# Pooled attention, then a gated two-layer net: late softmax sums of two heads in one matmul, and the engines' queues in another order

## The chip, the core and the metric

The kernel runs as one program on one core of a Trainium2 chip. Its engines are TensorE (PE, matmuls into PSUM), VectorE (DVE), ScalarE (ACT), GpSimd (POOL) and SyncE (SP, which issues the DMAs). They run side by side, each takes its own instructions in their order, and semaphores make one wait for another. The metric is the device time of a run in microseconds (us), as the median of several runs; lower is better. 0.3% of it is 2.6 us.

## What is computed

Four batches of eight heads of attention, 1152 keys, the queries averaged in pairs to 576; then every one of the 2304 rows of 512 numbers goes through a layer of 2048, a gate, and a layer back to 512. All is float32.

```
q_pool = q.reshape(B, H, S // 2, 2, D).mean(axis=3)         # B 4, H 8, S 1152, D 64
scores = (1 / sqrt(D)) * matmul(q_pool, k.transpose(0, 1, 3, 2))
attn = exp(scores - max(scores, axis=-1))
attn = attn / (sum(attn, axis=-1) + 1e-09)
x = matmul(attn, v)                                         # then rows of (B*S/2, H*D)
h = x @ w_in                                                # 512 -> 2048
out = (h * clip(h + 3.0, 0.0, 6.0) / 6.0) @ w_out           # 2048 -> 512
```

## The kernel before

**Groups and halves.** The attention is cut into 16 groups `g` (a batch and a pair of heads), and each group into two halves `h` of 288 queries. Within a half, `j` is the head of the pair. Scores stand with the keys on the 128 partitions, in nine blocks of 128 keys (`pqk`, L617, early groups `pv`, L613): a block is copied to SBUF by ACT, and DVE keeps the maximum over blocks (`m`). Groups 0 to 4 are "early" and use plain float32 scores; from group 5 on ("late") keys and queries are split in a high and a low part. The maximum over partitions goes through two small transposes on PE, `fold` and `spread` (L656 and L677 in the late form). Then DVE widens it (L649), subtracts it from the scores in three pieces a head (`s`, L688), ACT takes the exponential in place, POOL adds the nine blocks (`d`, L706), and PE multiplies with `v` (`pav`, L713, 36 matmul records a half).

**The late sums.** For each head, DVE's `turn_d` (L726) folds 288 sums of 128 partitions to 9 columns with 32 rows in each of four partition quarters. `sums` (L734) adds over the quarters with two matmuls into the same nine columns of PSUM: the matrix `same[:, 0]` puts head 0's total on partitions 0 to 63, `same[:, 1]` head 1's on 64 to 127. As float32 each is two records in the trace, four in all. Then, on DVE: `recip` (L762 adds 1e-9, L763 inverts), `widen_r` (L738), `divide` (L777). The tile `psr` that they work on takes the one PSUM buffer of tag `av` that the next half's `pav` needs.

**The net.** Its weights are split in two parts once, written to `w_d` in DRAM, and loaded again for each use (`w`, L375, half 0 for the first layer, half 1 for the second, three buffers each). x goes to DRAM as `xh_d` and `xl_d` (L791, "spill") and comes back by chunks of 256 rows (`mxmxh`, `mxmxl`, L382). A hidden step is 12 matmuls (`ph`, L392), then ACT, DVE (gate, L401), ACT and POOL; a projection step is 6 matmuls (`po`, L425). Six chunks of 16 steps run between the attention's matmuls; the last 768 rows run alone at the end: a chunk of 256 by `mxmxh` and `mxmxl`, and 512 rows in `last` (L907), for which the program's last part loads its weights by the same SP queue.

**The order.** Nothing is ordered by hand. `arrange` lists every step with a place in time, a cost on each engine that may run it, what it needs and which buffers it takes; `Order.run` walks through time and lets each free engine take the ready step with the least place. The constants at the top (`START`, `SLOPE`, `LAG`, `MLP`, `AT`, `ATL`, `PER`, `BIAS`, `CONV`, `CSTEP`, `STICK`) set the places; the costs stand in `arrange`. The resulting sequence is what the engines' queues hold: a queue waits at its next instruction, whatever stands behind it.

## Time and profile before

| | us |
| --- | --- |
| median of 3 runs | 880.97 |
| lowest and highest | 880.77, 883.16 |
| the profiled execution, its own time | 882.37 |
| span of its instructions | 880.6 |
| PE busy in the span | 841.0 |
| DVE, ACT, POOL busy | 671.9, 570.5, 496.5 |

The mean granted clock of PE is 0.99 of full speed. The profile shows the program in four parts: to about 175 us the early groups with the weights' conversion, then the late groups with six chunks of the net to about 707 us, then the end of the attention while the last chunk's x is under way, and from about 750 us the net alone.

### The profile page before, as it was taken

What the parts mean: (1) busy time and instruction counts of PE and PEld (TensorE: products, weight loads), DVE (VectorE), ACT (ScalarE), POOL (GpSimd) and SP (SyncE); (2) the same over time, 40 slices, a digit from 0 to 9 for tenths busy, and PEclk for the clock granted to TensorE, in tenths of its full rate; (3) what the DMA queues carried; (4) which work ended last, traced back from release to release, by engine and by line L of the source; (5) the groups of instructions that cost most, each with busy time, mean ns of one, the idle gap of its engine ahead of it and who ended that gap; (6) DMA issues with size and microseconds to landing.
All of it is one profiled execution on the core that took longest, in us unless ns stands there. A gap on an engine that the chain in (4) does not pass through costs nothing.

```text
span 880.6 us, 16285 instructions
## 1 busy us (share of the span) xinstructions
PE 841.0 (96%) x5712; PEld 653.7 (74%) x5712; DVE 671.9 (76%) x1313; ACT 570.5 (65%) x1203; POOL 496.5 (56%) x436
## 2 busy tenths in 40 slices
PE   4799999999999999999999999999999998999997
PEld 3445555577788887778888878888887876888886
DVE  4899999988988998888989887998888862222322
ACT  3779889886777786657767766776777652222222
POOL 2557775665768686828675767778676672000000
PEclk9899999999999999999999999999999999999999
DMA  9979596689787869969758778887767668533423
GB/s 244 318 215 284 176 287 219 226 276 322 273 258 253 252 242 282 299 206 311 242 188 259 243 239 273 288 239 258 243 240 250 216 211 265 186 120 120 144 96 96
DMA packets 114545, 206.06 MB, mean 234 GB/s; under 512 B 44576, under 2 KB 68128, under 8 KB 114464
## 3 DMA queue, kind: packets, MB, share of 16 engines
q1 hardware_dynamic: 113776, 203.65, 72.5%
q10 hardware_dynamic: 688, 1.38, 0.5%
q8 instruction: 45, 0.74, 0.3%
q14 instruction: 36, 0.29, 0.1%
HBM read 173.02 MB, written 31.98 MB: 233 GB/s over the span
## 4 chain that ended last, share of the span: by engine, by line
PE 71%; DVE 11%; DMA 7%; issue 5%; ACT 4%; POOL 1%; SPq 1%; DVEq 0%; POOLq 0%; ACTq 0%
PE ph L392 20%; PE po L425 15%; PE pav L713 12%; PE pqk L617 10%; PE pt L425 5%; DMA w<-w_d 4%; DVE m L635 4%; PE pv L613 3%; DVE s L688 2%; PE pt L591 1%; ACT s L522 1%; PE psr L744 1%; DVE kT L576 1%; DMA mxmxl<-xl_d 1%; DMA raw<-in_moe_w_in_dram 1%
## 5 line engine op out<-in xcount | busy, mean ns | idle before, releaser
L696 ACT ACTIVATE s<-s 128x864 f32<-128x864 f32 x192 | 177.5, 932 | 27.6 <-DVE s L688 25.9
L392 PE MATMUL ph<-mxmxh,w 128*128 128x256 f32 x896 | 182.4, 287 | 1.9 <-DVE r L401 1.0
L522 ACT COPY s<-pqk 128x288 f32<-128x288 f32 x396 | 145.4, 402 | 42.2 <-PE pqk L617 39.5
L688 DVE TENSOR_TENSOR s<-s,pst 128x864 f32<-128x864 f32 x167 | 172.0, 1042 | 0.5
L635 DVE TENSOR_TENSOR m<-pqk,m 128x288 f32<-128x288 f32 x308 | 137.3, 446 | 22.4 <-ACT s L522 14.8
L713 PE MATMUL pav<-s,vr 128*64 128x288 f32 x1152 | 153.4, 412 | 0.0
L392 PEld LDWEIGHTS ph<-mxmxh,w 128*128 128x128 f32 x896 | 147.4, 191 | 6.0 <-DVE r L401 2.5
L397 ACT ACTIVATE r<-ph,three 128x256 f32<-128x256 f32 (+1 forms) x128 | 64.0, 500 | 130.1 <-PE ph L392 124.0
L425 PE MATMUL po<-w,gh 128*128 128x512 f32 x448 | 140.3, 395 | 0.0
L401 DVE SCALAR_TENSOR_TENSOR r<-r,ph 128x256 f32<-128x256 f32 (+1 forms) x128 | 57.2, 447 | 97.6 <-ACT r L397 97.0
L392 PE MATMUL ph<-mxmxl,w 128*128 128x256 f32 x448 | 127.1, 284 | 1.0 <-DMA mxmxl<-xl_d 1.0
L410 POOL TENSOR_TENSOR gl<-r,gh 128x256 fp32r<-128x256 f32 x96 | 71.8, 748 | 92.2 <-ACT gh L405 88.0
L617 PE MATMUL pqk<-qh,kT 128*128 128x288 f32 x396 | 118.8, 315 | 2.1 <-ACT s L522 1.4
L713 PEld LDWEIGHTS pav<-s,vr 128*64 128x64 f32 x1152 | 77.3, 137 | 57.9 <-issue 10.7
L706 POOL TENSOR_TENSOR d<-s 128x864 f32<-128x864 f32 x44 | 90.3, 2053 | 51.5 <-ACT s L696 49.1
L617 PE MATMUL pqk<-ql,kT 128*128 128x288 f32 x396 | 111.6, 295 | 0.0
L425 PE MATMUL po<-w,gl 128*128 128x512 f32 x224 | 91.7, 409 | 6.8 <-DMA w<-w_d 4.7
L425 PEld LDWEIGHTS po<-w,gh 128*128 128x128 f32 x448 | 85.0, 190 | 14.6
L706 POOL TENSOR_TENSOR d<-d,s 128x864 f32<-128x864 f32 x44 | 90.3, 2053 | 1.7 <-ACT s L696 0.6
L392 PEld LDWEIGHTS ph<-mxmxl,w 128*128 128x128 f32 x448 | 85.7, 191 | 2.0 <-DMA mxmxl<-xl_d 1.2
L617 PEld LDWEIGHTS pqk<-qh,kT 128*128 128x128 f32 x396 | 75.1, 190 | 13.0 <-issue 3.1
L405 ACT CAST gh<-r 128x256 fp32r<-128x256 f32 (+1 forms) x128 | 55.8, 436 | 40.4 <-DVE r L401 37.4
(103 smaller groups left out, 1417.8 us busy)
## 6 DMA issues: line engine op xcount, KB each, us to landing
w<-w_d SPq DMA_DIRECT2D x224, 512.0 KB, 6.1
w_d<-scratch SPq DMA_DIRECT2D x32, 512.0 KB, 5.7
kr<-in_k_dram SPq DMA_DIRECT2D x32, 288.0 KB, 5.1
vr<-in_v_dram SPq DMA_DIRECT2D x16, 576.0 KB, 4.8
qr<-in_q_dram SPq DMA_DIRECT2D x15, 576.0 KB, 5.1
raw<-in_moe_w_in_dram SPq DMA_DIRECT2D x16, 512.0 KB, 4.9
raw<-in_moe_w_out_dram SPq DMA_DIRECT2D x16, 512.0 KB, 6.0
xh_d<-xh SPq DMA_DIRECT2D x32, 144.0 KB, 4.1
```

Source lines behind the costliest of these rows:

```text
L392: nc.tensor.matmul(ps, w[:, wi, cs], x[:, c, :], start=(m == 0), stop=(m == 3 * NCC - 1))
L397: nc.scalar.activation(out=r6, in_=ps, func=AF.Relu, bias=three)
L401: nc.vector.scalar_tensor_tensor(out=out, in0=r6, scalar=6.0, in1=ps, op0=ALU.min, op1=ALU.mult)
L410: on.tensor_tensor(out=gl, in0=r6, in1=gh.bitcast(F32), op=ALU.subtract)
L425: nc.tensor.matmul(o, g[:, ts], w[:, wi, :], start=(first and n == 0), stop=(last and n == 2))
L522: nc.scalar.copy(out=out, in_=in_)
L617: nc.tensor.matmul(ps[:, 0:HQ], kT[g][:, j, t, :], w[:, j, :], start=(m == 0), stop=(m == 1))
L635: nc.vector.tensor_tensor(out=m, in0=ps, in1=s0 if t == 1 else m, op=ALU.max)
L688: by[eng].tensor_tensor(out=s, in0=s, in1=m.unsqueeze(1).to_broadcast([P, KC, HQ]), op=ALU.subtract)
L696: nc.scalar.activation(out=s, in_=s, func=AF.Exp, scale=SCALE)
L706: by[eng].tensor_tensor(out=out, in0=x, in1=y, op=ALU.add)
L713: nc.tensor.matmul(av_t[g, h][j * D:(j + 1) * D, :], vr_t[g][:, j, t, :], s_t[g, h][:, j, t, :], start=(t == 0), stop=(t == KT - 1),)
```

## The change

Three things. `same` becomes one matrix of 128 by 128 that adds over the quarters for any column, and `sums` one matmul of 18 columns, nine of each head, so that every partition gets both heads' totals. `recip` adds 1e-9 to all 18 columns into a new tile, and inverts twice, on partitions 0 to 63 the nine columns of head 0, on 64 to 127 those of head 1. And all constants of the order are other numbers, with slightly other costs for some ten steps.

```diff
-        same = const.tile([P, 2, P], F32, name="same")
-        nc.vector.memset(same, 0.0)
-        for j in range(2):
-            nc.vector.tensor_reduce(
-                out=same[:, j, j * D:j * D + 32], in_=ident.rearrange("p (i k) -> p k i", k=32), axis=AX.X, op=ALU.add
-            )
-            nc.vector.tensor_copy(out=same[:, j, j * D + 32:j * D + 64], in_=same[:, j, j * D:j * D + 32])
+        same = const.tile([P, P], F32, name="same")
+        nc.vector.tensor_reduce(out=same[:, 0:32], in_=ident.rearrange("p (i k) -> p k i", k=32), axis=AX.X, op=ALU.add)
+        for i in range(1, 4):
+            nc.vector.tensor_copy(out=same[:, 32 * i:32 * (i + 1)], in_=same[:, 0:32])
...
-            for j in range(2):
-                nc.tensor.matmul(ps[:, HQ:HQ + NB], same[:, j], d[:, j], start=(j == 0), stop=(j == 1))
+            nc.tensor.matmul(ps[:, HQ:HQ + 2 * NB], same, d.rearrange("p j b -> p (j b)"), start=True, stop=True)
...
-            n, w = (P, NB) if g >= EARLY else (QP, 2 * TQ)
+            late = g >= EARLY
+            n, w = (P, NB) if late else (QP, 2 * TQ)
             den = d_t["r", g, h] = sm.tile([n, w], F32, tag=f"den{w}", name="den")
-            nc.vector.tensor_scalar(out=den, in0=d_t["p", g, h][:n, HQ:HQ + w], scalar1=EPS, scalar2=None, op0=ALU.add)
+            x = d_t["p", g, h][:n, HQ:HQ + 2 * w if late else HQ + w]
+            if late:
+                y = sm.tile([n, 2 * w], F32, tag="sum", name="sum")
+                nc.vector.tensor_scalar(out=y, in0=x, scalar1=EPS, scalar2=None, op0=ALU.add)
+                for j in range(2):
+                    nc.vector.reciprocal(out=den[j * D:(j + 1) * D], in_=y[j * D:(j + 1) * D, j * w:(j + 1) * w])
+                return
+            nc.vector.tensor_scalar(out=den, in0=x, scalar1=EPS, scalar2=None, op0=ALU.add)
             nc.vector.reciprocal(out=den, in_=den)
...
-ATL = (22.01, -2.54, -233.12, 551.12, 311.61, 236.17, 57.41, -176.29, 297.81, 167.8, 536.81, 237.72, 502.76, 92.46)
+ATL = (22.34, -3.63, -205.22, 577.83, 408.65, 315.01, 114.68, -312.66, 169.9, 228.56, 501.2, 268.78, 483.12, 159.04)
...
-                add(("rc", g, h), z, {"DVE": (345, 430)}, do("recip", g=g, h=h), [("de", g, h)])
+                add(("rc", g, h), z, {"DVE": (470, 560)}, do("recip", g=g, h=h), [("de", g, h)])
```

The new order shows at three places below. A row is an instruction, or some in a row, with its line (numbers differ by up to four in the new file), what it writes and reads, and the size of what it writes.

**SP's queue at the load of group 11's keys** (`kr`; `w` with a number are the net's weights, `xh_d` and `xl_d` the spill of a half). Before:

```order
L791 DMA xh_d<-xh 128x288
L791 DMA xl_d<-xl 128x288
L375 DMA w_5185<-w_d 128x1024
L506 DMA kr<-in_k_dram 128x9x64 x2
L375 DMA w_5218<-w_d 128x1024
L375 DMA w_5263<-w_d 128x1024
```

and now:

```order
L375 DMA w_5184<-w_d 128x1024
L375 DMA w_5214<-w_d 128x1024
L503 DMA kr<-in_k_dram 128x9x64 x2
L795 DMA xh_d<-xh 128x288
L795 DMA xl_d<-xl 128x288
L375 DMA w_5280<-w_d 128x1024
L375 DMA w_5301<-w_d 128x1024
```

The spill of a half stood two loads ahead of the keys and now stands right behind them, ahead of the weights. `w_5218` was for the second layer of the third chunk's step 9, `w_5280` is for that of step 8.

**DVE's queue at the last half of the attention**, from the widened maximum on (`pst<-pst`; `s` the three subtractions a head, `den`, `sum` and `psr<-den` the reciprocals of the half before, `x` its division, `r` a gate of the net). Before:

```order
L649 STREAM_TRANSPOSE pst<-pst 128x288
L688 TENSOR_TENSOR s<-s,pst 128x864 x3
L649 STREAM_TRANSPOSE pst<-pst 128x288
L688 TENSOR_TENSOR s<-s,pst 128x864 x2
L762 TENSOR_SCALAR den<-psr 128x9
L763 RECIPROCAL den<-den 128x9
L688 TENSOR_TENSOR s<-s,pst 128x864
L738 STREAM_TRANSPOSE psr<-den 128x288
L401 SCALAR_TENSOR_TENSOR r_9055<-r_9055,ph 128x256
L777 TENSOR_TENSOR x<-psr,x 128x288
```

and now:

```order
L646 STREAM_TRANSPOSE pst<-pst 128x288
L762 TENSOR_SCALAR sum<-psr 128x18
L764 RECIPROCAL den<-sum 64x9 x2
L401 SCALAR_TENSOR_TENSOR r_9045<-r_9045,ph 128x256
L734 STREAM_TRANSPOSE psr<-den 128x288
L685 TENSOR_TENSOR s<-s,pst 128x864
L781 TENSOR_TENSOR x<-psr,x 128x288
L685 TENSOR_TENSOR s<-s,pst 128x864 x2
L401 SCALAR_TENSOR_TENSOR r_9090<-r_9090,ph 128x256
L646 STREAM_TRANSPOSE pst<-pst 128x288
L685 TENSOR_TENSOR s<-s,pst 128x864 x3
```

The reciprocals of the half before, its division and a gate have moved from behind the subtractions to between the first of them.

**SP's queue at the end of the attention** (`last` the 512 rows, `out_dram` the sixth chunk's results; `w_9276` and `w_9278`, now `w_9297` and `w_9299`, are the net-alone part's weights for the first step's second layer and the second step's first layer). Before:

```order
L382 DMA mxmxl<-xl_d 128x4x256
L791 DMA xh_d<-xh 128x288
L791 DMA xl_d<-xl 128x288
L375 DMA w_9234<-w_d 128x1024
L907 DMA last<-xh_d 128x512
L907 DMA last<-xl_d 128x512
L375 DMA w_9276<-w_d 128x1024
L375 DMA w_9278<-w_d 128x1024
L439 DMA out_dram<-ob 64x512 x2
L439 DMA out_dram<-ob 32x512
L439 DMA out_dram<-ob 96x512
```

and now:

```order
L375 DMA w_9239<-w_d 128x1024
L795 DMA xh_d<-xh 128x288
L795 DMA xl_d<-xl 128x288
L375 DMA w_9297<-w_d 128x1024
L911 DMA last<-xh_d 128x512
L911 DMA last<-xl_d 128x512
L439 DMA out_dram<-ob 64x512 x2
L439 DMA out_dram<-ob 32x512
L439 DMA out_dram<-ob 96x512
L375 DMA w_9299<-w_d 128x1024
```

The weights of the first step's second layer have moved ahead of `last`, and those of the second step's first layer behind the four writes of results; the load of `mxmxl` stands some rows further ahead.

## Rows read from the trace of the kernel before

**Rows 1.** The page's part 1: each engine's busy time, share of the span, instructions.

```profile
PE 841.0 (96%) x5712; PEld 653.7 (74%) x5712; DVE 671.9 (76%) x1313; ACT 570.5 (65%) x1203; POOL 496.5 (56%) x436
```

**Rows 2.** Windows: stretch and length, busy time of each engine, clock, DMA.

```profile
175.00:200.00 25.00, 23.52 (x182) 18.07 (x183) 21.50 (x43) 19.48 (x43) 14.52 (x15) 0.93 0.85 278
200.00:700.00 500.00, 492.64 (x3419) 406.65 (x3419) 437.32 (x910) 356.15 (x826) 347.31 (x295) 1.00 0.80 257
700.00:760.00 60.00, 55.17 (x351) 44.14 (x347) 26.22 (x55) 23.17 (x46) 26.21 (x25) 1.00 0.68 220
...
380.00:400.00 20.00, 17.93 (x122) 14.55 (x121) 15.84 (x33) 12.75 (x28) 8.10 (x7) 0.91 0.83 252
```

**Rows 3.** Timeline of PE at 388: start, duration, instruction, [idle before <-releaser].

```profile
388.25 0.77 PE L425 MATMUL po<-w,gl 128*128 128x512 f32 x1 [2.08 <-POOL gl L410]
...
390.95 0.44 PE L617 MATMUL pqk<-qh,kT 128*128 128x288 f32 x1
```

**Rows 4.** Timeline of PE: the late sums of a half, and what follows.

```profile
717.52 0.51 PE L734 MATMUL psr<-dh,same 128*128 128x9 f32 x4
717.89 0.48 PE L425 MATMUL po<-w,gl 128*128 128x512 f32 x1
```

**Rows 5.** Groups by shape: line, instruction, count | busy us, mean ns | idle.

```profile
L734 PE MATMUL psr<-dh,same 128*128 128x9 f32 x88 | 11.2, 237 | 0.0
...
L677 PE MATMUL pst<-ident,mq 18*128 18x18 f32 x22 | 5.1, 233 | 0.0
...
L763 DVE RECIPROCAL den<-den 128x9 f32<-128x9 f32 x22 | 4.7, 216 | 0.8
```

**Rows 6.** Timeline of PE: last turns of group 10's keys, and a projection.

```profile
427.91 1.15 PE L557 MATMUL pt<-ident,kr 128*128 128x128 f32 x9
...
437.03 0.47 PE L425 MATMUL po<-w,gl 128*128 128x512 f32 x1 [0.32 <-DMA w<-w_d]
```

**Rows 7.** Timeline of SP's queue at the load of group 11's keys.

```profile
429.08 1.55 SPq L506 DMA_DIRECT2D kr<-in_k_dram  x2
430.68 6.11 SPq L375 DMA_DIRECT2D w<-w_d  x6
```

**Rows 8.** Chain that ended last: start, length, and whose work.

```profile
449.26 1.43 PE ph L392 x12
...
455.74 1.43 PE po L425 x6
458.31 4.52 PE pav L713 x36
```

**Rows 9.** Timeline of PE at the end of the attention.

```profile
706.76 0.30 PE L617 MATMUL pqk<-ql,kT 128*128 128x288 f32 x1
...
711.32 0.23 PE L677 MATMUL pst<-ident,mq 18*128 18x18 f32 x1
...
730.66 0.51 PE L734 MATMUL psr<-dh,same 128*128 128x9 f32 x4
...
748.77 0.28 PE L392 MATMUL ph<-mxmxh,w 128*128 128x256 f32 x1
```

**Rows 10.** Timeline of DVE in the last half of the attention.

```profile
712.12 2.98 DVE L688 TENSOR_TENSOR s<-s,pst 128x864 f32<-128x864 f32 x3
...
718.07 0.17 DVE L762 TENSOR_SCALAR den<-psr 128x9 f32<-128x9 f32 x1 [0.38 <-PE psr L734]
...
720.03 0.44 DVE L777 TENSOR_TENSOR x<-psr,x 128x288 f32<-128x288 f32 x1
...
728.95 0.47 DVE L726 TRANSPOSE_TENSOR_REDUCE dh<-d 128x9 f32<-128x288 f32 x1
```

**Rows 11.** Timeline of SP's queue at the end of the attention.

```profile
734.17 0.33 SPq L791 DMA_DIRECT2D xl_d<-xl  x1
...
739.57 0.32 SPq L907 DMA_DIRECT2D last<-xh_d  x1
...
743.24 2.26 SPq L439 DMA_DIRECT2D out_dram<-ob  x4
```

More of the change, by code (lines that the diff above doesn't have):

```diff
@@ L22 @@
 SWEEPS = ((0, 0, 8), (1, 0, 8), (0, 8, 16), (1, 8, 16), (2, 0, 16), (3, 0, 16), (4, 0, 16), (5, 0, 16))
-START = (297.45, 126.76, 394.29, 391.14, 380.14, 242.67, 333.14, 318.82)
-SLOPE = (-16.27, 2.59, -17.76, -9.21, 2.22, 26.51, 6.64, 17.68)
-LAG = 47.47
-MLP = (-344.5, 180.43, 24.29, -233.84)
-CONV = 259.96
-CSTEP = (428.74, 384.8)
+START = (246.01, 179.96, 358.36, 509.43, 415.86, 207.51, 251.46, 423.87)
+SLOPE = (-21.77, 9.37, -4.06, -18.53, 9.98, 26.0, 16.54, -0.66)
+LAG = 97.02
+MLP = (-392.54, 215.62, -17.55, -355.89)
+CONV = 309.52
+CSTEP = (368.54, 137.77)
 NEAR = 5
@@ L31 @@
 FCV = 12
-BIAS = (-117.79, -123.14, 79.41, -364.14, 39.25, 376.58)
+BIAS = (-634.41, -292.0, 59.75, -514.28, -65.55, 233.98)
 CUT = 8
-PER = (22.3, 20.22)
-AT = (216.76, -40.7, 3.26, 213.12, -263.52, 209.56, -146.85, 99.67, -205.13, 147.08, -190.26, -65.61, -218.54, 179.6)
-ATL = (22.01, -2.54, -233.12, 551.12, 311.61, 236.17, 57.41, -176.29, 297.81, 167.8, 536.81, 237.72, 502.76, 92.46)
+PER = (12.05, 21.32)
+AT = (287.65, -106.4, 1.62, 311.32, -328.57, 265.33, -319.67, 212.92, -55.41, 196.21, -167.72, -123.72, -327.69, 416.38)
+ATL = (22.34, -3.63, -205.22, 577.83, 408.65, 315.01, 114.68, -312.66, 169.9, 228.56, 501.2, 268.78, 483.12, 159.04)
 TAIL = 768
-STICK = 0.1993
+STICK = 0.2226
 CT = 256
@@ L179, in arrange @@
             if late:
-                add(("kl", g, c), z + 2 + c, {"DVE": (1130, 1130)}, do("keep_k", g=g, c=c), [("kh", g, c)], (), ("v" if g < NEAR else "s",))
+                add(("kl", g, c), z + 2 + c, {"DVE": (1178, 1160)}, do("keep_k", g=g, c=c), [("kh", g, c)], (), ("v" if g < NEAR else "s",))
         for h in range(NH if late else 1):
@@ L218, in arrange @@
                         p = (g, h)
-                        add(("tr", p), z + at[8], {"DVE": (665, 750)}, do("turn_m", u=p), [("mx", (g, h, n), KT - 1) for n in range(2)], (), ("m",))
+                        add(("tr", p), z + at[8], {"DVE": (700, 780)}, do("turn_m", u=p), [("mx", (g, h, n), KT - 1) for n in range(2)], (), ("m",))
                         add(("s1", p), z + at[2], {"PE": (110, 330, 0, "t")}, do("fold", u=p), [("tr", p)], ("st",))
-                        add(("s2", p), z + at[2], {"DVE": (430, 510)}, do("best", u=p), [("s1", p)])
-                        add(("s3", p), z + at[2], {"PE": (85, 300, 0, "t")}, do("spread", u=p), [("s2", p)])
+                        add(("s2", p), z + at[2], {"DVE": (485, 560)}, do("best", u=p), [("s1", p)])
+                        add(("s3", p), z + at[2], {"PE": (120, 320, 0, "t")}, do("spread", u=p), [("s2", p)])
                     if j:
                         for n in range(2):
-                            add(("tb", (g, h, n)), z + at[2] + n, {"DVE": (365, 450)}, do("widen_m", u=(g, h, n)),
+                            add(("tb", (g, h, n)), z + at[2] + n, {"DVE": (405, 498)}, do("widen_m", u=(g, h, n)),
                                 [("s3", p)] + [("su", (g, h, 0), c) for c in C3] * n)
@@ L242, in arrange @@
                 if late:
-                    add(("dt", u), z + at[7], {"DVE": (365, 450)}, do("turn_d", u=u), [("ad", u, 3)], () if j else ("dh",), ("d",))
+                    add(("dt", u), z + at[7], {"DVE": (392, 470)}, do("turn_d", u=u), [("ad", u, 3)], () if j else ("dh",), ("d",))
             y = z + at[5]
@@ L256, in arrange @@
             if late:
-                add(("de", g, h), z, {"PE": (200, 420, 0, "s")}, do("sums", g=g, h=h),
+                add(("de", g, h), z, {"PE": (190, 410, 0, "s")}, do("sums", g=g, h=h),
                     [("dt", (g, h, j)) for j in range(2)] + [("av", g, h, n)], ("av",), ("dh",))
-                add(("rc", g, h), z, {"DVE": (345, 430)}, do("recip", g=g, h=h), [("de", g, h)])
-                add(("rb", g, h), z, {"DVE": (365, 450)}, do("widen_r", g=g, h=h), [("rc", g, h)])
+                add(("rc", g, h), z, {"DVE": (470, 560)}, do("recip", g=g, h=h), [("de", g, h)])
+                add(("rb", g, h), z, {"DVE": (392, 482)}, do("widen_r", g=g, h=h), [("rc", g, h)])
             else:
```

## The prediction

> **What bounds the kernel now.** I read the page's busy times first: PE is busy for 841.0 of 880.6 us, the next engine, DVE, for 671.9 [rows 1]. So the time is PE's work and PE's waits, and the other engines count where PE waits for them. The windows say where it waits [rows 2]. From 200 to 700 us it is busy for 492.64 of 500, so 7.4 us are lost there; from 175 to 200, 1.5; from 700 to 760, 4.8. The worst of the middle is at 388 us, where PE stood for 2.08 us before a projection and then ran slow: the same score matmul that takes 0.30 takes 0.44 at 390.95 [rows 3], and the window from 380 to 400 has a granted clock of 0.91, near 1.8 us of 20 lost on top of the 2.07 of idleness [rows 2]. The early part, to 175 us, is no subject: all five queues hold the same rows in both kernels until the keys of group 5 are turned, but for the constants set up at the start, which lie under the first loads.
>
> All sums below are made on the profiled execution, span 880.6, own time 882.37. The median, 880.97, lies 0.4 above that span; I add the change of the span to the median.
>
> **The matmul.** Before, four records of the late sums take from 717.52 to 717.89, 0.37 us of PE's time [rows 4]; there are 22 halves (x88 records) [rows 5]. Now there are two records of 18 columns in place of four of 9. Do twice as many columns cost more? The trace has no such float32 product, but the nearest row, a small transpose of 18 columns, has a mean of 233 ns beside 237 for the 9 columns [rows 5], so the count of columns is not what costs here. I take half: 0.18 us each. The bounds are nothing saved, if 18 columns cost twice 9, and 0.2 each. Twenty of the 22 lie ahead of the last scores, where PE is the bound: 20 x 0.18 = **-3.6 us**. The last two stand in the end of the attention, where another chain decides (below): 0.
>
> The Trainium skill (TensorE: Matmul & The Clock Gate, Step-by-step: what each phase is for) says that streaming costs one cycle a column and that throughput is N cycles. By that rule alone one product of 18 columns would save nothing over two of 9, and the sum would be 3.6 us higher; the rows above, where 9 columns hold PE for about 90 ns a record, don't agree that columns are all.
>
> **The reciprocals.** DVE gets one more of 216 ns [rows 5] for each of 22 halves, on half the partitions each; bounds 0.1 and 0.22, so 2 to 5 us of DVE's time in all, I take 0.2 each. Behind it on DVE wait the widening, the division, and the maxima and subtractions of the next half; who waits in the end is the next `pav`, for the buffer that the division frees. In the new order at least 3.8 us of PE's work stand between a late sum and the next `pav`, and the work from the first reciprocal step to the division's end is 1.4 us (718.07 to 720.47 less a subtraction of 0.99, a third of the 2.98 at 712.12 [rows 10]), 1.6 with one more. So it costs 0 in the middle, and 0.2 where DVE is itself the chain, at the end. If that cover were gone it would be 22 x 0.2 = 4.4.
>
> **The end of the attention.** Before, PE goes from the last scores (706.76) to the spread of the maxima (711.32), to the last late sums (730.66), to the first layer of the second step of the net alone (748.77) [rows 9]: 4.6, 19.3 and 18.1 us. After that PE never waits. In the new order:
> - One hidden step and one projection, 1.43 and 1.41 [rows 8], have moved from behind the last scores to ahead of them: the last scores come 2.8 us later, and that much cover is gone.
> - From the last scores to the spread PE now has a whole `pav` (4.52), the fold, and one hidden step (1.43), with the changes between them some 6.5 us: +1.9.
> - From the spread to the late sums PE has only three projections, three hidden steps, one `pav` and one late sum: 3 x 1.41 + 3 x 1.43 + 4.52 + 0.2 = 13.2. But the chain is subtract, exponential, POOL's sums, fold to 9 columns. Before it took to 729.42 (the `dh` at 728.95 with its 0.47), 18.1 us [rows 10]. Now the reciprocals, the division and a gate, 1.6 us, stand among its first subtractions; some of that is lost in waits anyway and POOL has one step fewer among its sums, so +0.8, between 0 and +1.6: 18.9. PE waits about 5.5 us, in two or three pieces, and the late sums stand at 6.5 + 18.9 + 0.2 after the last scores, +1.7 on 23.9.
> - From the late sums on, 18.1 before: recip to spill 3.5 (734.17), 5.4 until the spill has landed and `last` is issued (739.57), then weights and writes [rows 9, 11]. Now the spill doesn't share the wires with the chunk's loads, which are issued rows earlier: 4 to 5.4. Then `last` (0.8), four writes (2.26 [rows 11]), and only then the weights of the second step, which land after 4 to 6.5. With 0.2 for the reciprocal: 3.7 + 0.8 + 2.3 and these bounds, 14.8 to 18.7; I take 16.8, -1.3. Half a microsecond of projection that stood behind is done by then: -0.5.
>
> Together 2.8 + 1.7 - 1.3 - 0.5 = **+2.7 us** (0 to +5).
>
> **The middle, 175 to 707 us.** The waits of before are tied to their order, so the 7.4 us and the slow stretch at 388 go, 9.2 in all. What is late next? I went along the new queues for chains whose cover, in PE's work, is shorter than what they took in the trace.
> - *Keys ahead of weights.* Before, the last turn of group 10's keys (427.91 to 428.9) frees the buffer for group 11's; its loads take 1.55 to issue from 429.08, the weights go out at 430.68, and PE waits for them until 437.03, 0.32 us [rows 6, 7]: 8.1 us from turn to landing against 7.8 of PE's work (two hidden steps and two projections, 5.7, the rest five pairs of scores, two small transposes and the changes between them). Now a spill's two issues of 0.33 [rows 11] stand between, 8.8; and PE has two hidden steps and one projection, 4.3, with six pairs of scores and a turn of queries, 2.2 like the rest of before: 6.5. Wait: 2.3, I take 2.2.
> - *The write of the third chunk's results* stands ahead of weights in the same way, with 6.6 us of PE's work from the projection that ends that chunk; scale, two writes and a load of some 6 make 8: 1.5.
> - *`pav` sooner after the exponentials.* In the second half of group 7 DVE has 14.6 us of rows from the widened maximum to the last subtraction, PE only 13.3 until the `pav` (the new order's rows at the durations of the trace, neighbours' overlap taken off); with the exponential 2.2 are missing. Three other halves miss 0.5 each.
> - *Two hidden steps close together* on the one PSUM buffer, three times: 0.8.
>
> That is 8.2; waits that no order shows (a load that lands late) and one slow stretch in two add 3. So 11.2 for 9.2: **+2 us**, and this is the softest term: 4 to 18 for 9.2, so -5 to +9.
>
> **The sum.** -3.6 + 2.7 + 2.0 = +1.1: the span goes to 881.7, the median to **882.1**.
>
> **Rivals.**
> 1. *The new queues run without knots.* For it: the middle loses only 1.5% as it is, and most of the chains that I followed in the new order have 2 us or more to spare. Then the middle loses 4 in place of 9.2, and the end 1 in place of 2.7: -3.6 + 1 - 5.2 = -7.8, some **874 to 878**, say 876 with part of it.
> 2. *Waits that slow the clock.* In the trace the wait of 2.08 us was followed by the half-speed stretch [rows 3]. The new order has three places with about 2 us or more: the second half of group 7, the weights behind group 11's keys, and the end. If two of them are followed by such a stretch of 1.8, and DVE's queue, full to 95% or more of PE's over the halves of groups 7 and 8, is late for a further 1 to 2: 882.1 + 5 = **887**. It decides from two stretches on. Against it: from 200 to 700 us the mean clock is 1.00 [rows 2], so the other 5.3 us of idleness there brought no second one.
> 3. *The product of 18 columns saves nothing.* All else as forecast, 882.1 + 3.6 = **885.7**. The rows of 18 and 9 columns speak against it.
>
> **How the numbers follow.** Within 0.3% of 880.97 (2.6 us, about what a measurement can tell from no change) is 878.3 to 883.6. The forecast has 0.42 and lies inside; rival 1 has 0.26, rival 2 has 0.27, rival 3 has 0.05. So faster 0.26, same 0.42, slower 0.32. The range for 8 in 10 takes in the likely parts of both first rivals: 875.5 to 888; the forecast's own is 879 to 884.
>
> **What would show it.** The late sums: 44 records, about 0.19 us from the first to what follows; four records' time would be rival 3. The window from 200 to 700: PE idle near 10 us is the forecast, 4 rival 1, and 14 with a granted clock under 0.99 rival 2. A wait of 2 us for a load of weights shortly after group 11's keys are issued, and none like the one at 388. At the end, waits of PE before the last `pav` and the last late sums of some 5 us together, and the second step's first layer 42 us after the last scores, as now. The forecast is wrong if PE's idle time in the middle halves or doubles, or if the end of the attention loses nothing.

## The result, and the profile after

The changed kernel takes **892.17 us** (median of 4 runs, 891.16 to 893.85), the kernel before 881.62 on the same chip: ratio 1.012, 95% interval 1.0096 to 1.0143. It is slower by 1.2%, some 10 us; the forecast was 882.1 with a range that ended at 888.0. The profiled execution took 891.56, its span 889.8 (880.6 before).

The page's first part, as [rows 1], each engine's busy time, share of the span and instructions:

```profile
PE 841.8 (95%) x5668; PEld 650.4 (73%) x5668; DVE 670.9 (75%) x1327; ACT 570.6 (64%) x1209; POOL 496.8 (56%) x437
```

The sums over the engines hardly differ. Of the 9.2 us of span, PE idles for 8.4 more (the span less PE's busy time: 48.0, 39.6 before), and stretches at a slower clock take part of the rest. The windows from 200 us on that answer to [rows 2], and two of 20 us (length, busy time of PE, PEld, DVE, ACT, POOL, granted clock, DMA share, GB/s):

```profile
200.00:700.00 500.00, 486.50 (x3333) 395.95 (x3332) 425.73 (x902) 347.54 (x810) 339.87 (x290) 1.00 0.78 253
700.00:760.00 60.00, 53.77 (x325) 43.80 (x325) 32.97 (x68) 27.23 (x58) 31.16 (x28) 0.94 0.71 232
440.00:460.00 20.00, 19.56 (x126) 16.12 (x127) 11.08 (x29) 9.17 (x26) 13.00 (x11) 0.91 0.70 240
740.00:760.00 20.00, 18.49 (x87) 15.63 (x88) 5.63 (x13) 5.03 (x11) 2.27 (x3) 0.87 0.67 218
```

From 200 to 700 us PE idles for 13.5 us, 7.4 before. The stretch at half clock (1.2 in place of 2.4 GHz) of 388 is gone, but there is one at 441 and a longer one at 739.

The late sums, as [rows 4] (TensorE's timeline: start, duration, instruction): two records, 0.14 us to what follows, where there were 0.37.

```profile
453.62 0.29 PE L730 MATMUL psr<-dh,same 128*128 128x18 f32 x2
453.76 0.47 PE L425 MATMUL po<-w,gl 128*128 128x512 f32 x1
```

So 18 columns in a record hold PE no longer than 9 do, and the matmul saves 0.22 us a half, a little more than the 0.18 of the forecast. The Trainium skill (TensorE: Matmul & The Clock Gate, Step-by-step: what each phase is for) has throughput as N cycles for N columns; at this size the trace does not agree.

The keys ahead of the weights, as [rows 6, 7], on TensorE and on SP's queue:

```profile
438.13 0.29 PE L614 MATMUL pqk<-ql,kT 128*128 128x288 f32 x1
440.44 0.47 PE L425 MATMUL po<-w,gl 128*128 128x512 f32 x1 [2.02 <-DMA w<-w_d]
...
442.16 0.45 PE L614 MATMUL pqk<-qh,kT 128*128 128x288 f32 x1
```

```profile
431.07 1.27 SPq L503 DMA_DIRECT2D kr<-in_k_dram  x2
432.44 1.25 SPq L795 DMA_DIRECT2D xh_d<-xh  x1
433.79 0.38 SPq L795 DMA_DIRECT2D xl_d<-xl  x1
434.22 4.51 SPq L375 DMA_DIRECT2D w<-w_d  x6
```

This wait was forecast at 2.2 and is 2.02, and the score matmul of 0.45 behind it shows the half clock. The half clock does not always come with the wait: of the kernels below, a2, a4, b3 and e1 have the same order there and wait for these weights for 1.3 to 2.0 us (in a2 and a4 the profile names POOL, but the projection starts 0.14 us after the weights land, as in the others), and none of them has a slow stretch behind it. What was not forecast is this, at 13 places in all: TensorE, then VectorE, then ScalarE at 343 us, in the second half of group 7 (`s` on VectorE the three subtractions, on ScalarE the exponential, `m` the maxima).

```profile
343.67 0.29 PE L614 MATMUL pqk<-ql,kT 128*128 128x288 f32 x1
345.11 0.40 PE L614 MATMUL pqk<-qh,kT 128*128 128x288 f32 x1 [1.15 <-DVE m L632]
...
345.57 1.68 PE L710 MATMUL pav<-s,vr 128*64 128x288 f32 x12
```

```profile
343.30 1.04 DVE L685 TENSOR_TENSOR s<-s,pst 128x864 f32<-128x864 f32 x1
344.26 0.46 DVE L723 TRANSPOSE_TENSOR_REDUCE dh<-d 128x9 f32<-128x288 f32 x1
344.64 0.42 DVE L632 TENSOR_TENSOR m<-pqk,m 128x288 f32<-128x288 f32 x1
```

```profile
344.44 0.94 ACT L693 ACTIVATE s<-s 128x864 f32<-128x864 f32 x1
```

A score block waits 1.15 us for a buffer that a maximum has to free, and the maximum stands behind a subtraction and a fold. Such a wait costs more than the profile lists: between the starts of these two rows lie 1.44 us, where blocks that wait for nothing start 0.13 apart, so 1.31 are lost and 1.15 listed. At the same time the half's last exponential ends at 345.37 and `pav` starts at 345.57. In the kernel before, the same half's last exponential and its `pav`:

```profile
347.20 0.95 ACT L696 ACTIVATE s<-s 128x864 f32<-128x864 f32 x1
```

```profile
366.39 1.68 PE L713 MATMUL pav<-s,vr 128*64 128x288 f32 x12
```

There 18 us lie between. Over the 22 late halves, from the same two rows of each, the median of that distance is 12.9 us before and 2.3 after; under 2 us are 2 halves before, 11 after. The new order has spent the cover that the chain of subtraction, exponential and `pav` had.

The end of the attention, as [rows 9, 10], on TensorE and on VectorE:

```profile
739.54 0.58 PE L730 MATMUL psr<-dh,same 128*128 128x18 f32 x2 [3.83 <-DVE dh L723]
739.96 0.77 PE L425 MATMUL po<-w,gl 128*128 128x512 f32 x1
```

```profile
737.31 0.48 DVE L723 TRANSPOSE_TENSOR_REDUCE dh<-d 128x9 f32<-128x288 f32 x1 [7.13 <-POOL d L703]
738.92 0.48 DVE L723 TRANSPOSE_TENSOR_REDUCE dh<-d 128x9 f32<-128x288 f32 x1 [1.13 <-POOL d L703]
```

The last late sums come 25.2 us after the last scores (739.54 less 714.33; 23.9 before, 25.6 forecast), with a wait of 3.8, and behind it the projection that took 0.48 takes 0.77.

### The profile page after: what moved, and what is told of

Its sections match the earlier page's. It is cut to its first block, busy times and chain, and to the rows that moved or that the text cites. A ratio compares the mean times of both kernels' runs of the same rounds, so it can differ in the third digit from the quotient of the medians.

```text
span 889.8 us, 16245 instructions
## 1 busy us (share of the span) xinstructions
PE 841.8 (95%) x5668; PEld 650.4 (73%) x5668; DVE 670.9 (75%) x1327; ACT 570.6 (64%) x1209; POOL 496.8 (56%) x437
## 4 chain that ended last, share of the span: by engine, by line
PE 63%; DVE 16%; DMA 6%; issue 5%; ACT 5%; POOL 4%; SPq 1%; DVEq 0%; POOLq 0%; ACTq 0%
PE ph L392 17%; PE po L425 12%; PE pav L710 12%; PE pqk L614 8%; DVE m L632 6%; PE pt L425 5%; DMA w<-w_d 4%; DVE s L685 3%; PE pv L610 3%; POOL d L703 3%; ACT s L519 2%; ACT s L693 1%; PE psr L740 1%; PE pt L554 1%; DMA raw<-in_moe_w_in_dram 1%
## 5 line engine op out<-in xcount | busy, mean ns | idle before, releaser
L392 PE MATMUL ph<-mxmxh,w 128*128 128x256 f32 x896 | 185.0, 289 | 2.4 <-DVE r L401 1.4
L685 DVE TENSOR_TENSOR s<-s,pst 128x864 f32<-128x864 f32 x168 | 174.0, 1042 | 0.6
L614 PE MATMUL pqk<-qh,kT 128*128 128x288 f32 x396 | 121.8, 321 | 8.8 <-DVE m L632 5.3
L425 PEld LDWEIGHTS po<-w,gh 128*128 128x128 f32 x448 | 84.9, 190 | 14.6
```

Of the source, the lines that this page charges most:

```text
L392: nc.tensor.matmul(ps, w[:, wi, cs], x[:, c, :], start=(m == 0), stop=(m == 3 * NCC - 1))
L425: nc.tensor.matmul(o, g[:, ts], w[:, wi, :], start=(first and n == 0), stop=(last and n == 2))
L614: nc.tensor.matmul(ps[:, 0:HQ], kT[g][:, j, t, :], w[:, j, :], start=(m == 0), stop=(m == 1))
L685: by[eng].tensor_tensor(out=s, in0=s, in1=m.unsqueeze(1).to_broadcast([P, KC, HQ]), op=ALU.subtract)
```

## The experiments

All times are medians. Each ratio is against the kernel before, run on the same chip at the same time, with its 95% interval. Since such medians of before lay between 880.2 and 882.3, the ratios compare better than the times.

| kernel | us | ratio | interval |
| --- | --- | --- | --- |
| changed kernel | 892.17 | 1.012 | 1.0096 to 1.0143 |
| a1, new sums, old order | 880.52 | 0.9993 | 0.9973 to 1.0013 |
| a2, old sums, new order | 890.71 | 1.0128 | 1.0095 to 1.0162 |
| b1, a1 without the addition | 878.63 | 0.9983 | 0.9959 to 1.0007 |
| b2, before with one more reciprocal | 884.35 | 1.0033 | 1.0015 to 1.0052 |
| b3, changed, fewer maxima | 887.72 | 1.0064 | 1.0039 to 1.0088 |
| b4, a1, fewer maxima | 874.96 | 0.9939 | 0.9914 to 0.9964 |
| h2, a1, new order 270 to 530 us | 888.27 | 1.0087 | 1.0061 to 1.0113 |
| h3, a1, new order 530 to 690 | 890.9 | 1.012 | 1.0093 to 1.0147 |
| h4, a1, new order from 690 | 886.2 | 1.0063 | 1.0038 to 1.0088 |
| h5, changed, old order 270 to 530 | 890.78 | 1.0105 | 1.0081 to 1.0129 |
| h6, changed, old order from 690 | 895.84 | 1.0155 | 1.0132 to 1.0178 |
| a3, changed, a load of weights earlier | 889.38 | 1.0106 | 1.0075 to 1.0136 |
| n1, a3, net steps into a run of scores | 891.94 | 1.0112 | 1.0091 to 1.0132 |
| a4, changed, last division later | 893.78 | 1.0152 | 1.0121 to 1.0182 |
| e1, changed, projection into the last wait | 890.12 | 1.0093 | 1.0071 to 1.0114 |
| c5, b1, two loads earlier | 875.82 | 0.9943 | 0.9923 to 0.9964 |
| c6, c5, copies ahead of the net | 877.41 | 0.9952 | 0.9934 to 0.997 |

### The two parts of the change, apart

a1 is the kernel before with the new `same`, `sums` and `recip`; its queues hold the old order, step by step. a2 is the changed kernel with the old three.

```diff
  a1, on the kernel before (same and recip as in the change); a2, on the changed kernel, the reverse:
-            for j in range(2):
-                nc.tensor.matmul(ps[:, HQ:HQ + NB], same[:, j], d[:, j], start=(j == 0), stop=(j == 1))
+            nc.tensor.matmul(ps[:, HQ:HQ + 2 * NB], same, d.rearrange("p j b -> p (j b)"), start=True, stop=True)
```

> The kernel before with only the matmul of 18 columns and the reciprocals by halves; every queue in the old order. Theory 1 (the order costs, the matmul gains): in the two traces four records of late sums of 9 columns take 0.362 us and two of 18 columns 0.14, so 20 halves in the middle save 4.4 us; the second reciprocal of each half lies under TensorE's work in the old order. 880.97 falls to 876 to 878, and TensorE's idle time from 200 to 700 us stays near 7.4. Theory 2 (the new sums and reciprocals delay VectorE and so cost themselves): 22 more reciprocals of 0.22 us each put VectorE's maxima late, at least half of what the matmul saves is given back as waits of score matmuls for m: 879 to 884.

> The changed kernel's order with the old two matmuls of 9 columns and one reciprocal on all partitions. Theory 1 (the order costs): the matmul's 4.4 us come back on top of 892.17: 895 to 898. Theory 2 (the extra reciprocal makes VectorE late): with it gone the waits of score matmuls for m, 5.3 us in the changed kernel, fall to some 2, and the time is 890 to 893 in spite of the two matmuls.

The order costs it: a2 is slower by 1.28%, 11.3 us, with the old sums. The new sums by themselves gain next to nothing: in the old order 0.6 us (a1, from 2.4 faster to 1.1 slower), in the new order 0.7 (1.012 beside a2's 1.0128), where PE's records save 20 x 0.22 = 4.4. Both times lie in the ranges of the second theories, but the waits that these named came only in part: score blocks wait for maxima for 1.7 us in a1 (0.4 before), which is not half of 4.4, and for 3.7 in a2, where some 2 were expected.

### What became of the matmul's saving

b1 leaves the addition of 1e-9 out, so that VectorE has two short steps a half, as before. b2 adds only one reciprocal to the kernel before. b3 and b4 leave out a quarter of the maxima.

```diff
  b1, on a1:
-                y = sm.tile([n, 2 * w], F32, tag="sum", name="sum")
-                nc.vector.tensor_scalar(out=y, in0=x, scalar1=EPS, scalar2=None, op0=ALU.add)
...
-                    nc.vector.reciprocal(out=den[j * D:(j + 1) * D], in_=y[j * D:(j + 1) * D, j * w:(j + 1) * w])
+                    x = d_t["p", g, h][j * D:(j + 1) * D, HQ + j * w:HQ + (j + 1) * w]
+                    nc.vector.reciprocal(out=den[j * D:(j + 1) * D], in_=x)
  b2, on the kernel before (late halves):
-            nc.vector.reciprocal(out=den, in_=den)
+                nc.vector.reciprocal(out=y[0:D], in_=den[0:D])
+                nc.vector.reciprocal(out=y[D:P], in_=den[D:P])
  b3, on the changed kernel, and b4, on a1, in most():
+            if u[0] >= EARLY and t in (4, 8):
+                return
```

> The old order with the matmul of 18 columns, and the two half reciprocals straight on PSUM, without the addition of 1e-9 (every sum is at least 1, so the float32 value is the same): VectorE has two short steps a half as before the change, 0.17 us less than with the addition. In the old order with the whole new recip the matmul's 4.4 us had gone into TensorE's work up to 430 us and came back later as waits of the score matmuls. Theory A (VectorE's extra 0.2 us a half is what the score matmuls wait for): without it the gain appears, 3 to 4.5 us under the kernel before, 876.5 to 878. Theory B (in that stretch the other engines' queues set the time whatever TensorE saves): 879.5 to 881.

> The kernel before, old order and old two matmuls of 9 columns, with only one more reciprocal on VectorE for each late half (the two halves of the partitions one after the other). Theory A (VectorE decides in the late halves): slower by 2.5 to 5 us, 883.5 to 886. Theory B (a reciprocal lies under TensorE's work in this order): 880 to 882.

> The changed kernel, with the maxima of the late scores' key blocks 4 and 8 left out: 88 steps of 0.448 us, 39 us less for VectorE, nothing less for TensorE. With the next kernel it gives the cost of the new order when VectorE has time to spare. Theory A (the new order costs because the score matmuls wait for VectorE's maxima): waits of pqk for m go from 5.3 to under 1 us, the time falls by 5 to 9, to 883 to 887, and is at most 6 above the old order with the same maxima left out. Theory B (the new order's cost is TensorE's own: loads, and the end of the attention): falls by under 3, and the distance between the orders stays at 10 to 12.

> The old order with the new sums and reciprocals, and the maxima of the late scores' key blocks 4 and 8 left out. Theory A (VectorE's lateness eats the matmul's gain in the old order): the gain of 4.4 us appears, 880.5 falls to 875 to 877. Theory B: 879 to 881, since the score matmuls find other waits.

One more reciprocal alone costs 0.33%, 2.9 us (1.3 to 4.6), as the first theory said: it does not lie under PE's work. How it reaches PE can be read where a score block waits for the maximum behind the reciprocals, on VectorE and TensorE, first in the kernel before:

```profile
675.50 0.21 DVE L763 RECIPROCAL den<-den 128x9 f32<-128x9 f32 x1
675.63 0.40 DVE L635 TENSOR_TENSOR m<-pqk,m 128x288 f32<-128x288 f32 x1
```

```profile
675.80 0.29 PE L617 MATMUL pqk<-ql,kT 128*128 128x288 f32 x1
676.08 0.40 PE L617 MATMUL pqk<-qh,kT 128*128 128x288 f32 x1
```

and in b2:

```profile
675.82 0.21 DVE L765 RECIPROCAL sum<-den 64x9 f32<-64x9 f32 x1
676.04 0.21 DVE L766 RECIPROCAL sum<-den 64x9 f32<-64x9 f32 x1
676.28 0.46 DVE L635 TENSOR_TENSOR m<-pqk,m 128x288 f32<-128x288 f32 x1
```

```profile
676.10 0.30 PE L617 MATMUL pqk<-ql,kT 128*128 128x288 f32 x1
676.80 0.40 PE L617 MATMUL pqk<-qh,kT 128*128 128x288 f32 x1 [0.40 <-DVE m L635]
```

Between the starts of the two score rows lie 0.28 us before and 0.70 in b2. The maximum starts 0.13 us after the start of the one reciprocal, but only when the second of the two is over. From the start of the addition to the end of the maximum it takes 0.72 us before and 1.12 in b2, in a1 and in the changed kernel (medians of the halves in which a maximum follows, 15 of the 22 in the old order). So the second reciprocal, of 0.21, puts VectorE back by 0.40 a half; why the row behind starts so late is not known.

In a1 VectorE's steps take as long as in b2. The matmul's 4.4 less b2's 2.9 would leave a gain of 1.5, which lies in a1's interval. So the second reciprocal accounts for most of what the matmul's saving lost. b1 is no test of a short `recip`: up to VectorE's next row it takes 0.44 us a half, 0.63 in a1 and 0.33 before. It lies 0.9 us from a1, which these runs cannot tell apart; that the addition is what a1 loses is not shown.

With 39 us less of maxima the old order gains 5.4 less 0.6, 4.8 us by the ratios, though PE's work is the same. So VectorE, busy for 437 of the 500 us from 200 to 700 [rows 2], sets part of the time there beside PE.

b3 says what the order's cost is *not*. It gains 4.9 us on the changed kernel, as much as the old order gained. Its waits for `m` (us, times, longest) have gone from 5.3 to

```profile
PE pqk L614 <- DVE m L634: 0.5, 1, 0.5
```

and yet PE idles for 12.3 of the 500 us, and b3 stands 1.25% behind b4, 11 us, as far as the orders stood apart with all maxima. Busy times and clock from 200 to 700 us, of b3:

```profile
200.00:700.00 500.00, 487.69 (x3369) 401.01 (x3368) 403.14 (x828) 350.57 (x820) 342.70 (x295) 1.00 0.78 256
```

### Where the new order costs

In h2 to h6 a program hands out the steps in the sequence of one order up to a point, then in that of the other; all else is the changed kernel.

```diff
-        for fn, eng in [(lambda eng: None, None)] + od.run():
+        order = od.run()
+        order = [order[i + k] for i, n in RUNS for k in range(n)]
+        for i, e in ENGINE.items():
+            order[i] = (order[i][0], e)
+        for fn, eng in [(lambda eng: None, None)] + order:
```

> New sums and reciprocals. All queues in the old order, but for the steps from score block 61 to 252 of the late ones, which stand in the new order: in time from about 270 to 530 us. In the two traces (old order with new sums, changed kernel) this stretch takes 255.0 and 264.9 us with the same work to within 0.3. Theory 1 (the knots seen in this stretch cost their lengths where they stand: loads behind keys, maxima and turned keys behind VectorE's queue): 6 to 9 above the 880.5 of the old order, 886.5 to 889.5. Theory 2 (what the new order costs is spread over the whole attention, by VectorE's load): 882 to 885.

> As the last, but only the steps from late score block 252 to 378 of 396 stand in the new order: from about 530 to 690 us. By the traces 160.3 and 167.3, of which 5.9 is work drawn ahead from behind (a product with v and a projection). Theory 1: +1, 880 to 883. Theory 2 (spread): 883 to 885.

> As the last, but only the steps from late score block 378 on stand in the new order: from about 690 us to the end of the attention. By the traces 186.2 and 186.7, though 4.5 of work have gone from it to the stretch ahead. Theory 1 (the end is a chain of its own: the late sums wait for the last fold, and the clock falls behind that wait): +3 to +5, 883.5 to 885.5. Theory 2 (the end costs what I forecast for it, and no clock): +1 to +2.7, 881.5 to 883.2.

> The changed kernel, but the steps from late score block 61 to 252, about 270 to 530 us, stand in the old order. Theory 1 (that stretch costs what its trace says, 255 in place of 265 us, and so over half of the whole): 892.2 falls by 6 to 8, to 884 to 886. Theory 2 (most of what such an exchange shows is made by the two changes between orders): 888 to 893.

> The changed kernel, but the steps from late score block 378 on, about 697 us, stand in the old order. Theory 1 (the end of the attention in the new order costs 4 to 5.7 by itself): 892.2 falls to 886.5 to 888.5. Theory 2 (the changes between orders made it): 890 to 893.

h2 came as the first theory said. In its trace the stretch takes 262.8 us, 255.0 in a1, with as many records of every kind (504 of `ph`, 258 of `po`). PE's waits from 270 to 530 us, of h2 (us, times, longest), show the waits of the changed kernel come along with the piece, where a1 waits for maxima once, for 0.2 us:

```profile
PE pqk L616 <- DVE m L634: 3.8, 8, 1.1
PE po L427 <- DMA w<-w_d: 1.2, 1, 1.2
PE pqk L616 <- DVE kT L575: 0.8, 1, 0.8
```

The others did not: h3, h4 and h6 are slower than either theory had them, and h5 gains 1.3 us where the first expected 6 to 8. A change between two orders makes knots of its own. In h3, and in the same way in h6, the late sums of the first half of group 15 wait until VectorE, behind two subtractions, has copied a product with `v` out of its PSUM buffer, and in h5 a projection waits for weights at the seam:

```profile
706.60 0.40 PE L732 MATMUL psr<-dh,same 128*128 128x18 f32 x2 [2.10 <-DVE x L523]
```

```profile
274.06 0.47 PE L427 MATMUL po<-w,gl 128*128 128x512 f32 x1 [2.54 <-DMA w<-w_d]
```

So these times are no measure of a piece, and part of h2's can be its seams too. The traces without a seam in the stretch are. Here is the time of TensorE between four of its rows, in the kernels that have the old order there (before, a1, b1, b2) and the new (the changed kernel, a2, a3, a4, e1, h5, leaving out those with an edit in the stretch):

| from, to | old order | new order |
| --- | --- | --- |
| last early scores, 61st late block | 99.4 to 100.8 | 94.7 to 96.8 |
| 61st, 253rd block | 255.0 to 257.4 | 262.0 to 264.9 |
| 253rd block, last late scores | 177.9 to 179.6 | 183.9 to 185.4 |
| last late scores, PE's last row | 167.2 to 170.8 | 168.8 to 170.0 |

The work in them is not the same. By PE's records the new order has a hidden step and a projection less in the first stretch (2.8 us), a hidden step more in the second (1.4; what is said ahead of h2 of the same work to 0.3 does not hold, 516 records of `ph` for 504), a hidden step and two projections more in the third (4.2), and a hidden step and a projection less in the last (2.8). Set against its work it gains about 1 us in the first, by the means, and loses about 5 in the second (8 in h2), 1 in the third and 3.5 in the last.

### Its knots, one by one

a3 moves one load on SP's queue; n1 moves, on top of it, a gate on VectorE and two steps of the net on TensorE. In these diffs `ahead` takes a step out of the planned list and puts it right in front of another.

```diff
  a3, n1:
+        ahead(("do_load_w", dict(m=(2, 8), n=1)), ("load_k", dict(g=11)))
  n1:
+        ahead(("do_gate", dict(m=(1, 9))), ("lessen", dict(u=(7, 1, 1), c=1)))
+        ahead(("do_layer", dict(m=(1, 10))), ("scores", dict(u=(8, 0, 1), t=6)))
+        ahead(("do_project", dict(m=(1, 9), first=False, last=False)), ("spread", dict(u=(8, 0))))
```

> The changed kernel with one load moved on SP's queue: the weights of the second layer of the third chunk's step 8, now behind group 11's keys and a spill, go ahead of them. Theory 1 (that wait costs its length and the slow stretch of 3.4 us at half clock behind it): the wait of 2.02 us at 438 goes and the clock of the window from 440 to 460, 0.91, goes to 1.00: 892.17 falls by 3 to 4, to 888 to 889. Rival a (another chain is late right behind it): TensorE only waits elsewhere, and less than 1 us is gained. Rival b (the slow stretch is not due to that wait): 2 us are gained, and the stretch stays or turns up elsewhere.

> The changed kernel with the weights ahead of group 11's keys, and at 340 to 354 us, where eleven score blocks stand with no step of the net between: the gate of the second chunk's step 9 on VectorE ahead of the second of three subtractions, and on TensorE the hidden step 10 ahead of the score block that waited 1.15 us, the projection of step 9 ahead of the spread that waited 0.64. Theory 1 (the wait is a matter of place: VectorE needs 1.04 for each subtraction and 0.45 for each maximum while TensorE needs 0.27 for a score block, and TensorE has nothing else to do): these two waits go, 889.4 falls by 1.5 to 3, to 886.5 to 888. Rival (the subtractions, now later, delay the product with v behind them by as much): 889 to 890, and pav waits in place of pqk and pst.

In a3 the wait of 2.02 is gone, with 0.40 of it left 1.7 us on, and no half clock stands here, as none stands in the runs that kept the wait:

```profile
440.00:460.00 20.00, 19.60 (x140) 16.03 (x140) 13.96 (x35) 11.83 (x32) 14.86 (x14) 1.00 0.75 251
```

The time fell by 2.8 us, by the ratios 1.2, and the intervals overlap. That a load in the wrong place was worth its wait is read from the trace and not shown by the runs, which only don't speak against it.

n1 is a miss, and tells more. The waits of 1.15 and 0.64 went, and these came (TensorE; then a window with the clock):

```profile
345.96 0.40 PE L614 MATMUL pqk<-qh,kT 128*128 128x288 f32 x1 [0.43 <-DVE m L632]
358.85 0.40 PE L614 MATMUL pqk<-qh,kT 128*128 128x288 f32 x1 [0.93 <-DVE m L632]
359.89 0.40 PE L614 MATMUL pqk<-qh,kT 128*128 128x288 f32 x1 [0.51 <-DVE m L632]
360.63 0.52 PE L614 MATMUL pqk<-qh,kT 128*128 128x288 f32 x1 [0.21 <-DVE m L632]
```

```profile
360.00:365.00 5.00, 4.79 (x23) 4.24 (x24) 4.69 (x10) 3.02 (x8) 2.87 (x3) 0.66 1.03 365
```

That is 2.1 us of waits where a3 has 1.8, and with the next one in both, 0.26 here and 0.55 in a3, it is 2.3 for 2.3. A stretch at half clock stands here too. So the wait was not a matter of place. It reads as if VectorE were behind by that much and PE met it later; no run takes work off VectorE at this place alone.

### The end of the attention

```diff
  a4:
+        for name in ("recip", "widen_r", "divide"):
+            ahead((name, dict(g=15, h=0)), ("lessen", dict(u=(15, 1, 1), c=2)))
...
+        ahead(("spill", dict(g=15, h=0)), ("lessen", dict(u=(15, 1, 1), c=2)))
  e1:
+        ahead(("do_project", dict(m=(5, 12), first=False, last=False)), ("sums", dict(g=15, h=1)))
```

> The changed kernel with the work of the half before the last (reciprocals, widening, division, split and spill) moved, on VectorE, ScalarE, GpSimd and SP's queue, from among the first subtractions of the last half to just ahead of the last of its subtractions, where the order of the kernel before has it. Theory 1 (this work stands in the chain from the spread to the last late sums): the wait of 3.84 us ahead of the last late sums shrinks by 1 to 1.6, and the time falls by 1 to 2 from 892.17. Rival (the last pav is then late for its buffer by as much, or it is the spill's landing that decides the end): no change within 0.5, or slower by up to 1.5.

> The changed kernel with one projection moved on TensorE from behind the last late sums into the wait of 3.84 us ahead of them. Theory 1 (the end is one chain, last fold, late sums, reciprocals, spill, loads of the last 512 rows: TensorE's work there lies under it): the wait shrinks to 2.4, the same 1.4 turns up as waits before the second step, and the time stays within 1 of 892.2. Theory 2 (TensorE's work and its clock set it): -1.4 with the projection, and up to -3 where the stretch of 6.8 us at half clock gets shorter too, 889 to 891.

a4 went as its rival said: its median is 1.6 us slower (2.8 by the ratios), though the intervals overlap. The wait for the last fold has not shrunk, the last `pav` now waits for the division, and a load of weights is late behind the later spill (TensorE):

```profile
729.81 4.59 PE L710 MATMUL pav<-s,vr 128*64 128x288 f32 x36 [0.99 <-DVE x L781]
740.01 0.58 PE L730 MATMUL psr<-dh,same 128*128 128x18 f32 x2 [4.00 <-DVE dh L723]
...
757.44 0.77 PE L425 MATMUL po<-w,gl 128*128 128x512 f32 x1 [3.32 <-DMA w<-w_d]
```

In e1 the projection fills part of the wait:

```profile
739.53 0.37 PE L730 MATMUL psr<-dh,same 128*128 128x18 f32 x2 [2.48 <-DVE dh L723]
741.09 0.58 PE L392 MATMUL ph<-mxmxh,w 128*128 128x256 f32 x1 [1.19 <-DVE r L401]
```

From the last scores on PE takes 167.65 us in place of 170.03, with the same 6.8 us at half clock. In the times it is 2.0 us, in the second theory's range, though the intervals overlap. So in the trace PE's work counts there, 1.4 of the 2.4, and the clock was not cured by a shorter wait (a3, with the wait at its full 3.84, has 3.4 us at half clock).

### A faster kernel

c5 is b1 with two loads of weights moved ahead of other transfers on SP's queue, at the two longest waits that b1's trace shows between 200 and 700 us; c6 moves four copies on ScalarE as well.

```diff
  c5, c6:
+        ahead(("do_load_w", dict(m=(1, 4), n=0)), ("load_k", dict(g=7)))
+        ahead(("do_load_w", dict(m=(2, 1), n=1)), ("do_write", dict(c=1, t=0, last=True)))
  c6:
+        for g, m in ((11, (3, 3)), (15, (5, 4))):
+            ahead(("keep", dict(u=(g, 0, 0), t=8)), ("do_relu", dict(m=m)))
+            ahead(("keep", dict(u=(g, 0, 1), t=0)), ("do_relu", dict(m=m)))
```

> The old order with the matmul of 18 columns and the reciprocals without the addition, and two loads of weights moved on SP's queue: that of the first layer of the second chunk's step 4 ahead of group 7's keys (TensorE waited 1.54 us for it at 252), that of the second layer of the third chunk's step 1 ahead of the four writes of results and group 9's v (2.05 us at 388, and the stretch at half clock behind). Theory: both waits go, with the stretch of 3.4 us: 878.6 falls by 3 to 5, to 873.5 to 875.6, the fastest of all so far. Rival: the buffers of these loads are not free any sooner or other transfers land later, so the waits turn up elsewhere: 877 to 879.

> The fastest so far (old order, matmul of 18 columns, reciprocals without the addition, two loads earlier), with ScalarE's copies of two score blocks, in groups 11 and 15, ahead of a step of the net that waits for its matmuls: TensorE waited 0.68 us twice for the second of these copies. If those waits just go, 875.8 falls by 0.8 to 1.4, to 874.4 to 875; if the delayed step of the net then holds up its gate and the next hidden step, no change.

c5 takes 875.82, faster than the kernel before by 0.57% (0.36 to 0.77) and the fastest here but for b4, which leaves maxima out. It lies just above the forecast of 873.5 to 875.6. On b1 it gains 3.5 us by the ratios, with intervals that still touch. Two of its windows:

```profile
200.00:700.00 500.00, 494.26 (x3423) 406.24 (x3422) 442.87 (x921) 360.60 (x834) 352.75 (x299) 1.00 0.80 256
380.00:400.00 20.00, 20.00 (x142) 16.69 (x142) 18.32 (x40) 15.66 (x37) 14.54 (x12) 1.00 1.02 327
```

The wait of [rows 3] and its slow stretch are gone; PE idles for 5.7 us from 200 to 700. The wait that the profile had put down to POOL at 388 was one for the weights: in that trace they landed at 388.11, the projection started at 388.25, and in c5, which asks for them sooner, nothing waits. c6 gained 0.16 us at each of its two places in the trace and nothing in the times.

## Why the prediction was wrong

Its sum was +1.1 for a span that grew by 9.2. The runs split the miss in two: the sums and reciprocals, put at -3.6, gave -0.6 (a1), and the order, put at +4.7, gave +11.3 (a2). By its own steps, on the two profiled traces:

- **The matmul, -3.6.** The records bear it out, -4.4. The row that it was judged by, the 233 ns of a small transposition, is a duration and does not say how long a record holds PE (90 ns of the 237 beside it), so that the half came out is luck in part. The step that failed is that these 20 halves lie "where PE is the bound", so that its saving is the kernel's: a1 has 0.6 us of it left. The Trainium skill (Perfetto Trace Analysis, Identifying the Most-Contended Engine) takes the engine with the highest occupancy as the one to work on, though it judges TensorE's headroom by other figures than its busy share. By busy share, PE's 95% beside VectorE's 76% spoke for PE. b2 and b4 show that VectorE's work counted as well.
- **The reciprocals, 0 in the middle.** Wrong: an extra one costs 2.9 us by b2, between the 0 taken and the 4.4 named as the price if the cover were gone. It puts VectorE back by 0.40 us a half and not by the 0.2 taken. The cover that I named was that of the next `pav`. What stands behind the reciprocals on VectorE, and is short, is the maxima that free the score buffers.
- **The middle, +2.0.** This is the term that was mis-sized most. With the matmul it was -1.6; the traces have +6.2 (their three stretches of the middle +9.0, less 2.8 of work moved in). The keys ahead of weights came out as worked out (2.02 for 2.2, 1.3 to 2.0 in other runs). The waits of `pav`, 3.7, and of the load behind the third chunk's results, 1.5, came nowhere. The score blocks' waits for maxima, 0.4 us before and 5.3 after over 13 places, were on no list. So it is not the working's merit that the idleness came near, 13.5 for about 10. It took chains one at a time, each by the durations of rows that had waited for nothing. The second half of group 7, where I had VectorE at 14.6 us for PE's 13.3, was the warning: I charged it to `pav`, and in n1 as much waiting came back when PE was sent elsewhere.
- **The end, +2.7.** The traces have +4.4 (1.6 from the last scores on, and the 2.8 moved). The last late sums stand as forecast, 25.2 us after the last scores for 25.6. What was left out is the clock, at half for 6.8 us around them in this execution. The gain of 1.3 that I took for the second step's loads is 0.4 (17.7 us for 18.1, to the row at 757.25).
- **The early part**, 0, had -1.4 in this pair; over all runs both orders lie between 169.5 and 172.8.

Rival 2 was nearest in kind: idleness of 13.5 us where it said 14, VectorE late by more than its "1 to 2", and slow stretches behind two of the three waits that it named. But the sign that it gave, a clock under 0.99 from 200 to 700, did not come (1.00), and the stretch at 441 stands in the profiled execution and not in a2, a4, b3 or e1, which have the same order there. Its price, 887, was 5 too low for want of the same term.

Not settled is one owner for the 5 to 8 us between 270 and 530. Maxima are not it alone (b3), nor one load (a3), nor the place of the net's steps (n1). What the traces show is the thin cover, 2.3 us for 12.9 between exponential and `pav`, and in n1 that waits taken away come back. That the first causes the second was not tried by itself.

## What to carry to other kernels

Where a second engine is busy for nine tenths of what the first is, in a stretch, a step taken off the first is not a gain until the second's queue is seen to allow it: add the step's cost to the second engine alone, and measure. Read an order by the distance between a producer's last step and its consumer on the bound engine; where its median fell from 13 us to 2 there were many short waits, not the two or three that can be followed by hand. Loads that stand behind other transfers on one queue are cheap to move: with two of them moved c5 is the fastest kernel here that does all the work, though its gain on b1 alone is not clear of the noise. And compare a wait and the clock behind it over several executions before one is put down to the other.

## What was not expected of the hardware

A float32 product of 18 columns, two records, held TensorE for 0.14 us; two products of 9, four records, for 0.36 to 0.37: the number of records was what cost here, not their columns. Each record comes with a weight load of its own, and the runs do not tell the two apart. A reciprocal over 64 partitions and 9 columns takes 0.21 us, as much as one over 128 (0.216), so halving the partitions doubled the cost. It more than doubled it for what stands behind: a maximum starts 0.13 us after the start of the one reciprocal, and 0.24 after that of the second half (medians). The stretches at half clock move between runs of like kernels: the one at 388 stood in the profiled execution of before and of b1, with the wait of 2.1 ahead of it, and neither in a1, where the wait was 0.58, nor in b2, where it was 1.45.
